# A transformer block on one core: filler matmuls between attention slots, and a new share of softmax tiles for VectorE

## The chip, the cores and the metric

The kernel runs on one core of one Trainium2 chip. The metric is the device time of one launch in microseconds (us), the median over several runs. A trace of one more execution, the profiled one, shows every instruction of the five engines: TensorE (PE, whose weight loads are listed apart as PEld), VectorE (DVE), ScalarE (ACT), GpSimd (POOL) and SyncE (SP, which here only issues DMAs).

## The reference

One pre-layernorm block over 2048 rows of width 640, in bf16: 32 heads of width 20, then a gated MLP of width 1728.

```python
h  = x + attention(layernorm(x), wqkv, wo)       # 32 heads, softmax over 2048 keys, scale 20**-0.5
n  = layernorm(h)
h2 = h + (gelu_tanh(n @ w_gate) * (n @ w_up)) @ w_down
```

## The kernel before

**Attention in tiles.** A tile is 128 x 512 scores in one bank of the sums' memory (eight banks of 512 f32). It comes from matmuls of 32 rows (line 965, `qk_mms`), is exponentiated, and goes into the output sums of its head through matmuls of 21 columns ("PV", built in `pv_op`, recorded under line 368 with `v_all` as an operand). Four tiles, one for each of four heads, are a *quad*. The queries are cut into eight chunks (`SIZES`: one of 512, five of 256, two of 128), and each chunk into *slots* of 64 tiles: 32 slots in all (0 to 7 for the first chunk, four for each chunk of 256, two for each of 128). All PV sums of a slot gather in bank 6. At the slot's end DVE copies them out (`osb`, line 1047, recorded under 368), four transposes (line 1057) and a few DVE operations finish them, and only after the copy may the next slot's first PV write to bank 6.

**Two engines make the exponentials.** Most tiles go to ACT, two or three tiles in one instruction (1024 or 1536 columns, written to `pts` or to `pts2`, which lies in `rege`). In each slot `D_QUADS` quads go to DVE instead (`d_exp`): one instruction at line 889 for each tile empties the bank into 16-bit integers, and a chain of five or six more (a polynomial in 16-bit arithmetic; a DMA that adds takes the place of one of them in most slots) works on two tiles at once before slot 18 ("narrow", 1024 columns) and on four from slot 18 = `D_WIDE` on ("wide", 2048 columns). `D_LEAD` says how many ACT tiles ahead of its place a DVE quad is begun; where it is zero (slots 0 to 8) the quads lie in the first `D_PART` of the slot.

**The rest is background.** The projections, and for each finished chunk the output projection, layernorm, gate (line 1138, emptied at 1173), GELU on ACT, up (1138 again, emptied at 1187) and down matmuls (1218, emptied at 1222) are placed wherever an engine is free. GELU and exp lie in different tables of ACT, so each group of GELUs between exps has a table load before and after it. The last chunk's part, after the last exp, is the *tail*.

**The order is made in advance.** All operations are recorded with an estimated duration, a priority and their dependencies; `Sched.schedule` plays them through once with these estimates, and each engine then runs its list strictly in the order that came out. An estimate that is changed moves operations in the lists; it changes no instruction. The scheduler also adds *filler matmuls* that compute nothing of use, when PE has nothing to do and its recent share of work falls under a bound (`WARM_MIN` of the last `WARM_WIN` = 3.4 us, `PAD_MIN` likewise). One filler kind multiplies zeros into bank 6 (four matmuls of 32 columns, `sc.pad`), possible before the change only while a slot's sums are being gathered (`live`). The other writes an idle bank (`sc.warm`, `self.spare`).

Of the kernel before, what the change touches and what calls it, by code (L numbers as in the profile page):

```python
# [18 lines left out]
WARM_WIN, WARM_MIN = 3.4, 0.5  # L19
# [27 lines left out]
class Sched:  # L47
# [13 lines left out]
    def op(self, eng, fns, dur, prio, reads=(), writes=(), acq=(), rel=(), after=(), sem=None, lat=None, mode=None, util=0.0):  # L61
        if eng == "dve" and rel and prio > self.ev:
            prio = self.ev
        o = Op()
        o.i = len(self.ops)
        o.eng, o.dur, o.lat, o.sem = eng, dur, DRAIN[eng] if lat is None else lat, sem
        o.util = util
        o.mode = mode
        o.tag = writes[0] if writes else None
        o.fns = fns if isinstance(fns, list) else [fns]  # L70
        o.prio = (prio, o.i)
        deps = set(after)
        for r in reads:
            if r in self.lw:
                deps.add(self.lw[r])
        for w in writes:
            if w in self.lw:
                deps.add(self.lw[w])
            deps.update(self.rd.get(w, ()))
        for r in reads:  # L80
            self.rd.setdefault(r, []).append(o.i)
        for w in writes:
            self.lw[w] = o.i
            self.rd[w] = []
        deps.discard(o.i)
        o.deps = deps
        o.acq = list(acq)
        o.rel = list(rel)
        o.succ = []
        o.ready = 0.0  # L90
        self.ops.append(o)
        return o.i

    def schedule(self):
# [5 lines left out]
        free_at = [0.0] * 8  # L100
        owner = [None] * 8
        last = [None] * 8
# [3 lines left out]
        mode = {e: None for e in ENGINES}  # L106
# [5 lines left out]
        order = []  # L112
        t = 0.0
        recent = collections.deque()
        live = False
        due = None
        total = len(ops)
        while done < total:
            assert events, "no operation can start"
            t = heapq.heappop(events)  # L120
            while events and events[0] <= t + 1e-9:
                heapq.heappop(events)
            for e in ENGINES:
                while future[e] and future[e][0][0] <= t + 1e-9:
                    _, p, i = heapq.heappop(future[e])
# [6 lines left out]
                while ready[e]:  # L132
                    p, i = heapq.heappop(ready[e])
                    o = ops[i]
# [40 lines left out]
                if chosen is None:  # L175
                    if e == "pe" and self.warm is not None:
                        while recent and recent[0][0] < t - WARM_WIN:
                            recent.popleft()
                        b = next((b for b in self.spare if owner[b] is None and free_at[b] <= t + 1e-9), None)
                        free7 = b is not None and all(hasattr(ops[d], "fin") and ops[d].fin + 0.06 <= t for d in self.warm_deps)  # L180
                        if sum(x for _, x in recent) < WARM_MIN * WARM_WIN and (free7 or live):
                            o = Op()
                            o.i, o.eng, o.lat = len(ops), "pe", DRAIN["pe"]
                            o.prio, o.sem, o.tag, o.util = (9, 0), None, "warm", 0.213
                            o.acq, o.rel, o.succ, o.dur = [], [], [], 0.215
                            if live and (mode[e] == "col" or not free7):
                                o.fns, o.mode, o.deps = list(self.pad), "col", set()
                            else:
                                o.fns, o.mode = [self.warm[b]], "full"
                                o.deps = set(self.warm_deps) | ({last[b]} if last[b] is not None else set())  # L190
                                last[b] = o.i
                            ops.append(o)
                            chosen = o
                            total += 1
                    if chosen is None:
                        continue
                o = chosen
                if e == "pe" and o.tag and o.tag[0] == "S":
                    self.spare = self.spares[o.tag[1]]
                if e == "pe" and self.pad is not None and o.tag and o.tag[0] in ("O", "OD"):  # L200
                    s_ = o.tag[1] if o.tag[0] == "O" else o.tag[1][0]
                    self.left[s_] -= 1
                    live = self.left[s_] > 0
                    while recent and recent[0][0] < t - PAD_WIN:
                        recent.popleft()
                    u = sum(x for _, x in recent) + o.util
                    room = due - t - MODE_SWITCH[e] if due is not None and due > t else 1e9
                    while u < PAD_MIN * PAD_WIN and o.util < 1.1 and o.dur + 0.215 < room and (live or o.tag[0] == "O"):
                        o.fns = o.fns + self.pad
                        o.dur += 0.215  # L210
                        o.util += 0.213
                        u += 0.213
# [120 lines left out]
DA_ISSUE, DA_LAT = 0.95, 7.0  # L333
DA_SLOTS = (1, 2, 3, 5) + tuple(range(9, 32))
PR, PR2 = 12, 6
D_QUADS = (1,) + (2,) * 15 + (2, 2) + (3,) * 10 + (2, 2, 2, 2)
D_FIRST, D_PART = 2, 0.75
D_LEAD = ((0,) * 8, (0, 10, 20) + (42,) * 21)
D_WIDE = 18
RSQRT_MAGIC = float(0x5F3759DF)  # L340

# [1 line left out]
P_QK, P_PV, P_PRO, P_EPI, P_LN, P_BG = 0, 1, 1.5, 2, 2.5, 3  # L343
# [3 lines left out]
def bass_sequential_preLN__mha_block__glu_gated_geglu__prompt_kernel(  # L347
# [12 lines left out]
    with ExitStack() as es:  # L360
        sc = Sched(nc)
        op = sc.op
# [4 lines left out]
        def I(method, *args, **kwargs):  # L367
            return lambda eng: getattr(eng, method)(*args, **kwargs)  # L368
# [64 lines left out]
        wg = carve(NA * DFF).rearrange("p (a f) -> p a f", a=NA)  # L433
        wu = carve(NA * DFF).rearrange("p (a f) -> p a f", a=NA)
# [55 lines left out]
        def cst(fn, key, n=128):  # L490
# [7 lines left out]
           reads=["zer"], writes=["qf1"])  # L498
        op("act", I("activation", f32(qt_all[:, 2, :, :]), zer[:, 0:2].bitcast(FP32).to_broadcast([128, 2048]), ACT.Copy), 1.8, P_QK,
           reads=["zer"], writes=["qf2"])  # L500
        op("act", I("activation", v_all[:, :, :, DH], zer[:, 0:1].unsqueeze(2).to_broadcast([128, NT, H]), ACT.Copy, bias=1.0), 0.5, P_QK,
           reads=["zer"], writes=["vones"])
# [28 lines left out]
        def load(dst, src, key, mb, after=(), writes=None):  # L531
            return op("sp", I("dma_start", dst, src), 0.08, P_BG, writes=writes or [key], after=after,
                      sem=key, lat=mb)
# [85 lines left out]
                   rel=[bk], after=after)  # L619

        def dma_transposes(src, rkeys, dst, wkey, after=()):
            op("sp", I("dma_start_transpose", dst, src), 1.25, P_EPI, reads=rkeys, writes=[wkey], sem=f"xp{wkey[1]}", lat=2.0, after=after)

        _id = [0]

# [182 lines left out]
        slot_end = []  # L808
        lead = sum(D_LEAD, ())
        for s_, (c, gs) in enumerate(slots):  # L810
            nk = 512 // CHUNKS[c][1]
            quads = [(s_, g, kb) for g in gs for kb in range(NT // nk)]
            n = D_QUADS[s_]
            taken = [quads[len(quads) * (m + 1) // (n + 1)] for m in range(n)]
# [432 lines left out]
        for s_, (c, gs) in enumerate(slots):  # L1247
            if c == 0:
                g = s_
                if g + 1 in STEP:  # L1250
                    t, (g0, g1) = g + 1, STEP[g + 1]
                    pr = P_EPI if t == 1 else P_BG
                    proj_q(t, 0, BG0, pr)
                    proj_k(t, BG0, pr)
                    q_bound(0, (t - 1, t), g0, g1, BG0, pr)
                if g < 3:
                    for kt in range(NT * g // 3, NT * (g + 1) // 3):
                        proj_v(kt, 1, BG0, P_BG)
                if g == 5:
                    prefetch(0)  # L1260
                if g >= 5:
                    cc = g - 4
                    for t in range(NA):
                        proj_q(t, cc, BG0, P_BG)
                    q_bound(cc, tuple(range(NA)), 0, NG, BG0, P_BG)
                if g == 7:
                    wr = tuple(w_readers)
                    load(wg, B_w_gate.rearrange("(a p) f -> p a f", p=128), "wg", 11.0, after=wr)
                    load(wu, B_w_up.rearrange("(a p) f -> p a f", p=128), "wu", 16.0, after=wr)
                    load(wd[:, 0:NF - 1, :], B_w_down[0:(NF - 1) * 128, :].rearrange("(a p) d -> p a d", p=128),  # L1270
                         "wd", 21.0, after=wr)
                    r0 = (NF - 1) * 128 - F0[-1]
                    load(wd[r0:128, NF - 1, :], B_w_down[(NF - 1) * 128:DFF, :], "wd", 2.6, after=wr)
                    op(POOL, I("memset", wd[0:r0, NF - 1, :], 0.0), 0.8, P_BG, writes=["wdz", "pool"], after=wr)
            while ui < len(units) and begins[ui] < slot_end[s_]:
                unit(ui)
                ui += 1
            if gs[-1] == NG - 1:
                tail = c == len(CHUNKS) - 1
                sc.ev = P_EV  # L1280
                post(c, ALLB if tail else BGF[c + 1], ALLB if tail else BGC[c + 1], tail)
                if not tail:
                    prefetch(c + 1)
# [30 lines left out]
```

## Time and profile before

| | us |
|---|---|
| median of 3 runs (915.36 to 915.76) | 915.65 |
| the profiled execution, whole | 915.13 |
| its span from the first to the last instruction | 913.0 |
| ACT busy | 871.2 |
| PE busy | 832.7 |
| DVE busy | 763.3 |
| POOL busy | 134.2 |

The 2.1 us between the profiled time and its span lie outside the trace, and that execution was 0.5 us faster than the median. Busy times are unions: neighbouring instructions of one engine overlap a little, so durations of single instructions add up to more. Instructions made through the helper in line 368 all carry that line, and are told apart by their tiles.

### The profile page before, as it was taken

What the parts mean: (1) busy time and instruction counts of PE and PEld (TensorE: products, weight loads), DVE (VectorE), ACT (ScalarE), POOL (GpSimd) and SP (SyncE); (2) the same over time, 40 slices, a digit from 0 to 9 for tenths busy, and PEclk for the clock granted to TensorE, in tenths of its full rate; (3) what the DMA queues carried; (4) which work ended last, traced back from release to release, by engine and by line L of the source; (5) the groups of instructions that cost most, each with busy time, mean ns of one, the idle gap of its engine ahead of it and who ended that gap; (6) DMA issues with size and microseconds to landing.
All of it is one profiled execution on the core that took longest, in us unless ns stands there. A gap on an engine that the chain in (4) does not pass through costs nothing.

```text
span 913.0 us, 25152 instructions
## 1 busy us (share of the span) xinstructions
PE 832.7 (91%) x11135; PEld 383.4 (42%) x11180; DVE 763.3 (84%) x1426; ACT 871.2 (95%) x786; POOL 134.2 (15%) x239
## 2 busy tenths in 40 slices
PE   3999999998897887899998989999999999999998
PEld 2432222222243332334443443344444445666667
DVE  8869989988798985777887989989999998958643
ACT  7999899999999999999999999999999999999971
POOL 5001110000013111111321101031102110203000
PEclk9999999999999999999999999999999999999999
DMA  7213344346304231242422324433353344314300
GB/s 259 84 31 79 79 87 108 96 96 203 127 1 76 48 59 24 48 68 59 91 51 50 64 39 85 91 62 71 78 107 62 70 81 98 47 26 85 56 9 23
DMA packets 52500, 68.05 MB, mean 75 GB/s; under 512 B 20892, under 2 KB 38392, under 8 KB 52392
## 3 DMA queue, kind: packets, MB, share of 16 engines
q0 software_dynamic: 12960, 33.56, 20.4%
q1 hardware_dynamic: 39432, 32.89, 13.2%
q8 instruction: 87, 1.43, 0.6%
q14 instruction: 21, 0.17, 0.1%
HBM read 20.12 MB, written 8.09 MB: 31 GB/s over the span
## 4 chain that ended last, share of the span: by engine, by line
ACT 68%; PE 19%; DVE 7%; DMA 2%; POOL 2%; issue 1%; SPq 0%
ACT pts L368 43%; ACT rege L368 24%; PE ps L965 5%; PE ps L667 4%; PE ps L1138 3%; PE ps L368 3%; PE ps L1218 3%; DMA regw<-in_A_wqkv_dram 1%; ACT L368 1%; DVE qt_all L368 1%; DVE rege L889 1%; DVE qt_all L889 1%; DVE dwx L368 1%; POOL nw L368 1%; DVE rege L368 1%
## 5 line engine op out<-in xcount | busy, mean ns | idle before, releaser
L368 ACT ACTIVATE pts<-ps 128x1536 bf16<-128x1536 f32 (+1 forms) x468 | 556.1, 1352 | 5.1 <-PE ps L965 2.7
L965 PE MATMUL ps<-qt_all,kt_all 32*128 32x256 bf16 (+2 forms) x4096 | 315.0, 274 | 42.6 <-ACT pts L368 25.5
L368 ACT ACTIVATE rege<-ps 128x1536 bf16<-128x1536 f32 (+1 forms) x232 | 289.7, 1359 | 5.5 <-PE ps L368 3.8
L965 PEld LDWEIGHTS ps<-qt_all,kt_all 32*128 32x128 bf16 x4096 | 108.6, 92 | 252.6 <-ACT pts L368 130.5
L1138 PE MATMUL ps<-rege,regw 128*128 128x256 bf16 (+2 forms) x1103 | 158.0, 274 | 9.6 <-DVE rege L1187 3.6
L368 PE MATMUL ps<-pts,v_all 128*21 128x256 bf16 (+2 forms) x2338 | 124.5, 276 | 0.4 <-ACT pts L368 0.3
L1138 PEld LDWEIGHTS ps<-rege,regw 128*128 128x128 bf16 x1120 | 85.9, 98 | 61.4 <-issue 27.0
L889 DVE TENSOR_SCALAR rege<-ps 128x512 int16<-128x512 f32 x120 | 82.3, 686 | 19.6 <-PE ps L965 18.7
L368 PE MATMUL ps<-rege,v_all 128*21 128x256 bf16 (+2 forms) x1358 | 91.8, 280 | 0.4 <-DVE rege L368 0.2
L889 DVE TENSOR_SCALAR qt_all<-ps 128x512 int16<-128x512 f32 x116 | 79.5, 686 | 12.0 <-PE ps L965 11.1
L667 PE MATMUL ps<-regw 128*128 128x512 bf16 (+1 forms) x345 | 84.2, 351 | 4.7 <-DMA regw<-in_A_wqkv_dram 1.6
L1218 PE MATMUL ps<-regw,rege 128*128 128x320 bf16 x448 | 78.1, 301 | 1.7 <-DVE rege L1222 0.8
L368 DVE TENSOR_TENSOR qt_all<-qt_all 128x2048 int16<-128x2048 f16 (+3 forms) x79 | 74.2, 940 | 1.0
L368 PEld LDWEIGHTS ps<-pts,v_all 128*21 128x21 bf16 x2338 | 53.9, 91 | 32.3 <-issue 26.9
L368 DVE TENSOR_SCALAR qt_all<-qt_all 128x2048 int16<-128x2048 int16 (+3 forms) x111 | 63.5, 574 | 1.0
L1187 DVE TENSOR_TENSOR rege<-rege,ps 128x512 bf16<-128x512 bf16 (+1 forms) x53 | 35.8, 678 | 23.7 <-PE ps L1138 21.8
L368 DVE TENSOR_TENSOR rege<-rege 128x1024 f16<-128x1024 f16 (+1 forms) x74 | 50.6, 684 | 0.9
L1218 PEld LDWEIGHTS ps<-regw,rege 128*128 128x128 bf16 x448 | 37.4, 97 | 30.5 <-issue 13.6
L368 DVE TENSOR_SCALAR rege<-rege 128x1024 int16<-128x1024 int16 (+2 forms) x112 | 48.3, 439 | 2.2 <-DMA rege<-qt_all 1.0
L368 PE MATMUL ps<-kt_all,zer 128*32 128x512 bf16 x576 | 49.5, 390 | 0.0
L667 PEld LDWEIGHTS ps<-regw 128*128 128x128 bf16 x360 | 28.1, 99 | 45.8 <-issue 24.4
L368 PEld LDWEIGHTS ps<-rege,v_all 128*21 128x21 bf16 x1358 | 36.0, 91 | 21.7 <-issue 14.2
(114 smaller groups left out, 785.4 us busy)
## 6 DMA issues: line engine op xcount, KB each, us to landing
qt_all<-qt_all POOLq DMA_DIRECT2D x11, 512.0 KB, 5.1
qt_all<-dwx POOLq DMA_DIRECT2D x11, 512.0 KB, 5.8
rege<-rege POOLq DMA_DIRECT2D x16, 256.0 KB, 3.6
rege<-dwx POOLq DMA_DIRECT2D x8, 512.0 KB, 5.3
dvx<-qt_all POOLq DMA_DIRECT2D x8, 512.0 KB, 4.6
rege<-in_A_x_dram SPq DMA_DIRECT2D x5, 640.0 KB, 5.8
q_rows<-regw SPq DMA_DIRECT2D x20, 128.0 KB, 1.9
out_dram<-rege SPq DMA_DIRECT2D x16, 160.0 KB, 2.6
```

The costliest lines, as they stand in the source:

```text
L368: return lambda eng: getattr(eng, method)(*args, **kwargs)
L667: yield op("pe", lambda eng, l=l, r=r, k=k: eng.matmul(bank(bk, n), l, r, start=(k == 0), stop=(k == len(steps) - 1)), c_mm(n) + cold, pri ...
L889: d_ops.append(op("dve", lambda eng: eng.tensor_scalar(v[:, 512 * h:512 * h + 512], bank(b), EXP_MUL, -32000.0, ALU.mult, ALU.max), c_dve( ...
L965: return lambda eng: eng.matmul(out()[:, kk * nq:(kk + 1) * nq], kt_all[32 * j:32 * j + 32, g, kt * 128:(kt + 1) * 128], qt_all[32 * j:32 ...
L1138: op("pe", lambda eng, a=a, f=f, fi=fi: eng.matmul(bank(bk)[:, fi * nq:(fi + 1) * nq], w[:, a, F0[f]:F0[f] + 128], hnT[:, a, 128 * tb:128 ...
L1187: hdone.append(op("dve", lambda eng, bu=bu, fv=fv, w=w: eng.tensor_tensor(fv, fv, bank(bu, w), ALU.mult), c_dve(w), p, reads=[ku] + hkeys( ...
L1218: op("pe", lambda eng, f=f, o=o, hf=hf, bk=bk: eng.matmul(bank(bk, 320), ha_f[:, o:o + 128], wd[:, f, hf * 320:(hf + 1) * 320], start=(f = ...
```

## The change

The zero matmuls may now also be placed between two slots, when bank 6 has been copied out and the next slot's first PV has not come (`free6`, after the first PV of the kernel, `begun`). The DVE quads are spread anew: three instead of two in slots 13 and 15; from slot 18 on a pattern of 3, 3, 2 in place of ten slots with three and four with two; 74 quads instead of 73. They are begun 36 tiles ahead instead of 42, and lie in the first 65% of the slots 0 to 8 instead of 75%. Three estimates of DMA times are longer: a transposing DMA 2.8 us for 2.0, the loads of the gate and up weights 12.0 and 17.5 us for 11.0 and 16.0.

```diff
-        live = False
+        live = begun = False
...
                         free7 = b is not None and all(hasattr(ops[d], "fin") and ops[d].fin + 0.06 <= t for d in self.warm_deps)
-                        if sum(x for _, x in recent) < WARM_MIN * WARM_WIN and (free7 or live):
+                        free6 = begun and not live and owner[6] is None and free_at[6] <= t + 1e-9
+                        if sum(x for _, x in recent) < WARM_MIN * WARM_WIN and (free7 or live or free6):
...
                             if live and (mode[e] == "col" or not free7):
                                 o.fns, o.mode, o.deps = list(self.pad), "col", set()
+                            elif free6 and (mode[e] == "col" or not free7):
+                                o.fns, o.mode, o.deps = list(self.pad), "col", {last[6]}
+                                last[6] = o.i
...
-                    live = self.left[s_] > 0
+                    live, begun = self.left[s_] > 0, True
...
-D_QUADS = (1,) + (2,) * 15 + (2, 2) + (3,) * 10 + (2, 2, 2, 2)
-D_FIRST, D_PART = 2, 0.75
-D_LEAD = ((0,) * 8, (0, 10, 20) + (42,) * 21)
+D_QUADS = (1,) + (2,) * 11 + (2, 3, 2, 3, 2, 2) + (3, 3, 2) * 3 + (3, 3, 2, 3, 2)
+D_FIRST, D_PART = 2, 0.65
+D_LEAD = ((0,) * 8, (0, 10, 20) + (36,) * 21)
...
         def dma_transposes(src, rkeys, dst, wkey, after=()):
-            op("sp", ..., 1.25, P_EPI, reads=rkeys, writes=[wkey], sem=f"xp{wkey[1]}", lat=2.0, after=after)
+            op("sp", ..., 1.25, P_EPI, reads=rkeys, writes=[wkey], sem=f"xp{wkey[1]}", lat=2.8, after=after)
...
-                    load(wg, ..., "wg", 11.0, after=wr)
-                    load(wu, ..., "wu", 16.0, after=wr)
+                    load(wg, ..., "wg", 12.0, after=wr)
+                    load(wu, ..., "wu", 17.5, after=wr)
```

In the changed file four lines are added ahead of most of the code, so line 368 becomes 372, 889 becomes 893, 965 becomes 969, 1138 becomes 1142, 1218 and 1222 become 1222 and 1226.

## The prediction

> **What bounds the kernel now.** I read the page first, then the clock and the engines in short stretches, ACT's own timeline with its idle times, and the chain of the last 50 us.
>
> ```profile
> PE 832.7 (91%) x11135; PEld 383.4 (42%) x11180; DVE 763.3 (84%) x1426; ACT 871.2 (95%) x786; POOL 134.2 (15%) x239
> ACT 68%; PE 19%; DVE 7%; DMA 2%; POOL 2%; issue 1%; SPq 0%
> ```
>
> ACT is busy 95% and holds 68% of the chain that ended last. Its timeline has no idle time worth naming between 40 and 876 us, except in a few places; these are the longest (idle time and releaser in brackets):
>
> ```profile
> 95.34 2.37 ACT L368 ACTIVATE rege<-ps 128x1536 bf16<-128x1536 f32 x2 [2.77 <-PE ps L368]
> ...
> 199.14 2.37 ACT L368 ACTIVATE rege<-ps 128x1536 bf16<-128x1536 f32 x2 [0.98 <-PE ps L368]
> ...
> 302.21 4.62 ACT L368 ACTIVATE pts<-ps 128x1536 bf16<-128x1536 f32 x4 [1.05 <-PE ps L368]
> 570.10 1.02 ACT L368 ACTIVATE pts<-ps 128x1024 bf16<-128x1024 f32 x1 [0.80 <-PE ps L965]
> 571.32 2.37 ACT L368 ACTIVATE pts<-ps 128x1536 bf16<-128x1536 f32 x2 [0.19 <-PE ps L965]
> 595.02 2.60 ACT L368 ACTIVATE rege<-ps 128x1536 bf16<-128x1536 f32 x2 [1.00 <-PE ps L965]
> 598.49 2.37 ACT L368 ACTIVATE pts<-ps 128x1536 bf16<-128x1536 f32 x2 [0.86 <-PE ps L965]
> ```
>
> The last four, 2.85 us, belong together. Cut into stretches of 2 us (columns: PE, PEld, DVE, ACT, POOL busy with counts, granted clock, DMA share, GB/s), the granted clock is 1.00 except here and, for 6.8 us, from 590.9:
>
> ```profile
> 564.00:566.00 2.00, 1.48 (x24) 0.54 (x22) 2.00 (x5) 2.00 (x3) 0.00 (x0) 1.00 0.00 0
> 566.00:568.00 2.00, 1.63 (x22) 0.82 (x22) 2.00 (x4) 2.00 (x3) 0.85 (x1) 0.75 0.03 8
> 568.00:570.00 2.00, 2.00 (x30) 0.60 (x18) 1.29 (x4) 1.30 (x1) 0.32 (x1) 0.50 0.67 131
> ```
>
> Both dips begin at the end of a slot (DVE copies `osb` at 564.44 and 591.18), after a stretch in which PE has almost only score matmuls. With half the clock PE falls behind ACT.
>
> After the last exp (876.3 us) the chain is PE's:
>
> ```profile
> 874.65 3.23 PE ps L1138 x32
> ...
> 894.78 3.81 PE ps L1218 x28
> 898.58 7.11 PE ps L1138 x127
> 905.69 0.02 issue
> 905.71 0.43 DVE rege L1163
> 906.14 0.05 issue
> 906.19 3.99 PE ps L1218 x28
> ```
>
> So there are two limits: ACT until 876 us, then, for 34 us, the matmuls that PE has left. A gain must take time from ACT before its last exp, or matmuls from behind it.
>
> **The change part by part.** The order of the changed program's instructions gives the counts; prices come from the rows of before.
>
> *ACT's own work.* Exps of 1024 columns fall from 344 to 342, those of 1536 stay at 356 (one more quad on DVE). A 3+2 pair of tiles repeats every 2.26 us; a third tile costs 1563 - 1139 = 424 ns; that leaves (2.26 - 0.42)/2 = 0.92 us for one of 1024. Gain 1.84 us. But the GELU of 1792 columns (chunk 6), which ran in the tail at 881.4 us for 1.70 us, now stands before the last exps, after another GELU group: +1.65. Net **-0.2** before the last exp. Table loads fall from 16 to 14, at 1.28 us each; both that vanish were in the tail, where ACT waits 1.6 to 5.6 us at a time for others: counted at nothing. If ACT were the tail's bound they would give 2.6.
>
> *Early slots, 65% for 75%.* A two-quad slot has 56 ACT tiles; the last DVE tile moves from 0.94 x 0.75 x 56 = 39 to 34 tiles, 5 tiles earlier, each 2.26/5 = 0.45 us: 2.4 us. The idle times at the ends of slots 1, 2 and 5 (2.77, 0.42, 0.21 and 0.98) come from there: the DVE copy of bank 6 stands behind chain work, the next slot's PV waits for the copy, and ACT for the score buffers that PV would free. Of these 4.4 us a shift of 2.4 would take 4.0 (2.4 off the first, the rest whole); but what moves forward meets other DVE work (22.8 us of 25 busy from 75 to 125), so the bound on the other side is nothing. I take the middle, **-2.2**.
>
> *Clock.* The changed order has 52 of its 620 zero matmuls between slots (none of 576 before), and 66 full-width ones for 62. Eleven more groups of four, 0.28 us each by 843.60 to 844.15 (eight in 0.55), are 3 us of PE, and four wide ones at 0.22 another 0.9. They go where PE waits: its weight loads wait 191 us in all for ACT to free a bank (130.5 and 60.9). So nothing on the path; without that cover, 3.9. If both dips go, 2.85 us return. But by columns times the share of the array they use, matmuls filled 0.45 of the 3.4 us before the first dip, and a dozen other such stretches at 0.45 or less kept the clock; a new order may dip elsewhere, at about 1.4 us a time. Two thirds: **-1.9**, bounds -2.85 and +1.4.
>
> The Trainium skill ("TensorE: Matmul & The Clock Gate", section "HAM oscillation — how this bites in real kernels") warns only of PE gaps of more than about 3.4 us; the trace halves the clock after waits of PE of at most 0.56 us, with PE busy 1.48 of 2.00 us. Here the trace decides; what the rule would make of the pads is the second rival.
>
> *DVE.* Two more narrow quads, one wide less. Narrow: 4 x 0.686 to empty the banks, two chains of 3 x 0.42 and 2 x 0.684: 8.0 us. Wide: 2.74 + 3 x 0.687 + 2 x 1.216 = 7.2. Net +8.8 us on 763, with three more adding DMAs on POOL's queue (about 0.9 us each of a POOL busy 15%). Slots 12 to 17 take it: by instruction lists times durations they go from 139 to 150 us of DVE work, against 148 us of ACT time; from slot 18 on the sum stays (352 and 354), but it no longer presses ten slots in a row, where DVE was busy 23.8 to 24.9 of each 25 us (600 to 750). Nothing for that as long as DVE's lateness stays inside the lead; two slot ends, 13 and 15, are newly full, and three patterns later: I allow **+1.5**, about two waits of the size of 0.66 and 1.05 seen at slot 9.
>
> *Lead 36 for 42.* Six tiles, 2.7 us less between a quad's start and its use. The last tile of a three-quad slot is begun 36 + 0.04 x 52 = 38 tiles, 17 us, before the slot ends; after it come 4.5 us of chain, about 5 us of adding DMA (4.6 to 5.8 for 512 KB), and queueing. Nothing, within those 7 us of slack; beyond them, the first rival.
>
> *The tail.* Behind the last score matmul stand 25 matmuls of 1138 with 256 columns fewer (all of them), 20 fewer of 128 columns (200 for 220), and 107 of 1218 for 112. Prices: 7.11/127 = 0.056, (3.23 - 7 x 0.056)/25 = 0.113, 3.9/28 = 0.14. 2.8 + 1.1 + 0.7 = 4.6 us, which PE does before the last exp instead; there its weight loads wait 11.4 us for ACT between 750 and 876 us, which hides it. What comes late next is DVE: between output projection and the last transposes PE had 23 + 46 matmuls of cover (5.7 us) and now has 20 + 25 (4.2), while the layernorm chain there took 5.3 us to its last instruction, 0.4 of it behind an emptying. At worst PE waits 1.3 us; at best two stops of 0.57 us behind line 1222 (880.5, 884.0) go too. Bounds -3.3 and -5.7; I take **-4.0**.
>
> *Longer estimates.* They only reorder; the transposing DMA took 3.3 us in the trace, the loads 10.7 and 15.7. SP issues 181 instructions before and after, and one store and one prefetch change places. Nothing.
>
> Sum: -0.2 - 2.2 - 1.9 + 1.5 - 4.0 = -6.8. Profiled 915.13 gives 908.3; the median stood 0.5 higher: **908.8 us**.
>
> **The rivals.** *Too short a lead (slower).* At a slot's end its last DVE quad is not ready, PE's queue stands at that PV, the copy and the next PVs follow, and ACT runs out of score buffers: the 2.77 us mechanism, now in slots 11 to 31. For it: 2.7 us less lead, and DVE near full there. Against: with 42, saturated DVE made hardly any such wait after slot 10. If half of the 21 slot ends pay the mean of the four slot-end waits (2.77, 0.42, 0.98, 1.05: 1.3 us), that is 14 us, in place of the allowance: 908.8 - 1.5 + 14 = 921. It decides from 8.3 us on, six such ends.
>
> *The clock does not follow the pads.* By the skill's rule they would buy nothing, since no gap of PE came near 3.4 us. The dips stay and one more comes: 908.8 + 1.9 + 0.7 (half a dip) = 911.4. For it: the dozen thin stretches that kept it show that padding is not the whole condition. Against: both dips lie exactly in unpadded slot ends.
>
> *The tail's gain is paid before it.* PE's extra background and pads in the last 125 us meet score matmuls; half of the 4.6 us returns as ACT idle time, and the early waits stay: 908.8 + 2.3 + 2.2 = 913.3, and with one dip more 914.7: no change.
>
> **How the numbers follow.** Chances: the forecast with its bounds (905 to 911) 0.42; better than that (early waits -4.0, clock -2.85, tail -5.7: 904.4) 0.10; clock 0.17; gain paid back 0.14, of which 0.08 lands within 0.2% (1.8 us, about what a measurement tells from no change); too short a lead 0.17. Faster: 0.42 + 0.10 + 0.17 + 0.06 = 0.75; same 0.08; slower 0.17. The range takes in all but the far end of the lead rival and the last of the good case: 903.5 to 917. The faster cases alone span 903.5 to 913.3.
>
> **What would show it.** Right: last exp ends near 873.5 us, span's end 32.7 us after it (36.7 before); granted clock 1.00 at slot ends; ACT idle after slots 1, 2 and 5 under 2 us in sum. Wrong: ACT idle times behind PE L372 (PV) after slot 12; half clock in other places; in the tail, PE waiting for DVE's layernorm operations before the last transposes.

## The result, and the profile after

The changed kernel takes **910.8 us** (median; 909.7 to 912.4) against 915.5 us for the kernel before beside it: a ratio of 0.9957, 95% interval 0.9942 to 0.9972. It is faster by 0.43%; the forecast was 908.8 us. In a later set of runs (experiment 5) the ratio was 0.9968 (0.9955 to 0.9980).

The profiled execution took 910.32 us, its span 908.4 us, 4.6 us less than before. From the page:

```profile
PE 831.5 (92%) x11183; PEld 386.0 (42%) x11228; DVE 768.4 (85%) x1445; ACT 867.3 (95%) x782; POOL 133.3 (15%) x242
ACT 55%; PE 28%; DVE 14%; POOL 3%; issue 1%; DVEq 0%
```

ACT's timeline, every start with a wait of 0.4 us or more between 45 and 880 us (bracket: idle time and releaser):

```profile
55.72 4.63 ACT L372 ACTIVATE pts<-ps 128x1536 bf16<-128x1536 f32 x4 [1.04 <-PE ps L372]
97.25 2.37 ACT L372 ACTIVATE rege<-ps 128x1536 bf16<-128x1536 f32 x2 [2.70 <-PE ps L372]
...
149.95 3.28 ACT L372 ACTIVATE pts<-ps 128x1024 bf16<-128x1024 f32 x3 [1.04 <-PE ps L372]
...
618.73 1.02 ACT L372 ACTIVATE pts<-ps 128x1024 bf16<-128x1024 f32 x1 [2.23 <-PE ps L372]
642.81 4.63 ACT L372 ACTIVATE pts<-ps 128x1536 bf16<-128x1536 f32 x4 [0.47 <-PE ps L372]
...
801.02 2.37 ACT L372 ACTIVATE pts<-ps 128x1536 bf16<-128x1536 f32 x2 [0.61 <-PE ps L969]
```

In this execution the two clock dips are gone. The same places, the ends of slots 19 (563.5) and 20 (589.2), in stretches of 2 us (PE, PEld, DVE, ACT, POOL, clock, DMA share, GB/s):

```profile
564.00:566.00 2.00, 1.98 (x30) 0.99 (x31) 0.82 (x2) 2.00 (x3) 0.00 (x0) 1.00 0.00 0
566.00:568.00 2.00, 2.00 (x35) 0.91 (x24) 0.59 (x3) 2.00 (x3) 0.00 (x0) 1.00 0.00 0
...
590.00:592.00 2.00, 1.98 (x30) 0.93 (x31) 2.00 (x4) 2.00 (x3) 0.00 (x0) 1.00 0.66 228
```

And the chain at the end, which is PE's again:

```profile
875.77 1.33 PE ps L1222 x9
877.10 0.56 PE ps L1142 x10
877.65 0.56 PE ps L372 x32
...
890.19 3.81 PE ps L1222 x28
893.99 7.11 PE ps L1142 x127
901.10 0.02 issue
901.12 0.43 DVE rege L1167
901.55 0.05 issue
901.60 3.99 PE ps L1222 x28
```

Where 32 matmuls of line 1138 stood between the last score matmul and the last PV, there are now 9 down matmuls and 10 of the gate or up kind with 128 columns. **Nothing was won before the last exp: it ends at 877.3 us, 1.05 us later than before. The whole gain lies behind it: 31.1 us to the end of the span, 36.7 before.** The waits of ACT of 0.15 us and more between exps sum to 9.9 us, before 9.8. The 2.85 us of the dips came back as other waits, first of all 2.23 us at the end of slot 21.

### The profile page after: what moved, and what is told of

The parts are those of the page before. It is cut to its first block, busy times and chain, and to the rows that moved or that the text cites. A ratio compares the mean times of both kernels' runs of the same rounds, so it can differ in the third digit from the quotient of the medians.

```text
span 908.4 us, 25274 instructions
## 1 busy us (share of the span) xinstructions
PE 831.5 (92%) x11183; PEld 386.0 (42%) x11228; DVE 768.4 (85%) x1445; ACT 867.3 (95%) x782; POOL 133.3 (15%) x242
## 4 chain that ended last, share of the span: by engine, by line
ACT 55%; PE 28%; DVE 14%; POOL 3%; issue 1%; DVEq 0%
ACT pts L372 34%; ACT rege L372 19%; PE ps L969 8%; PE ps L372 5%; PE ps L671 5%; PE ps L1142 5%; PE ps L1222 4%; DVE dwx L372 3%; DVE qt_all L372 2%; DVE rege L893 1%; DVE qt_all L893 1%; POOL nw L372 1%; DVE rege L1109 1%; ACT L372 1%; DVE stats L372 1%
## 5 line engine op out<-in xcount | busy, mean ns | idle before, releaser
L372 ACT ACTIVATE pts<-ps 128x1024 bf16<-128x1024 f32 (+1 forms) x467 | 552.9, 1330 | 7.0 <-PE ps L372 5.5
L969 PE MATMUL ps<-qt_all,kt_all 32*128 32x256 bf16 (+2 forms) x4096 | 314.2, 272 | 39.6 <-ACT pts L372 19.2
L372 ACT ACTIVATE rege<-ps 128x1024 bf16<-128x1024 f32 (+1 forms) x231 | 284.5, 1328 | 3.5 <-PE ps L372 3.1
L1142 PE MATMUL ps<-rege,regw 128*128 128x256 bf16 (+2 forms) x1101 | 154.5, 272 | 8.8 <-DVE rege L1191 3.6
L372 PE MATMUL ps<-pts,v_all 128*21 128x256 bf16 (+2 forms) x2330 | 122.0, 275 | 0.6 <-ACT rege L372 0.5
L893 DVE TENSOR_SCALAR rege<-ps 128x512 int16<-128x512 f32 x124 | 84.8, 686 | 15.6 <-PE ps L969 14.9
L372 DVE TENSOR_TENSOR qt_all<-qt_all 128x1024 int16<-128x1024 f16 (+3 forms) x81 | 74.7, 922 | 1.1
L372 PE MATMUL ps<-kt_all,zer 128*32 128x512 bf16 x620 | 54.8, 386 | 0.3 <-DVE osb L372 0.3
L372 POOL DMA_DIRECT2D qt_all<-dwx x25 | 23.0, 921 | 169.2 <-DVE dwx L372 158.6
```

The costliest lines, as they stand in the source:

```text
L893: d_ops.append(op("dve", lambda eng: eng.tensor_scalar(v[:, 512 * h:512 * h + 512], bank(b), EXP_MUL, -32000.0, ALU.mult, ALU.max), c_dve( ...
L969: return lambda eng: eng.matmul(out()[:, kk * nq:(kk + 1) * nq], kt_all[32 * j:32 * j + 32, g, kt * 128:(kt + 1) * 128], qt_all[32 * j:32 ...
L1142: op("pe", lambda eng, a=a, f=f, fi=fi: eng.matmul(bank(bk)[:, fi * nq:(fi + 1) * nq], w[:, a, F0[f]:F0[f] + 128], hnT[:, a, 128 * tb:128 ...
```

## The experiments

Each ran beside the kernel before on the same chip. "Tail" in the expectations is mostly the time from the last exp to the span's end. The table at the end of this section counts from the start of the last score matmul, which is the cleaner mark. "Waits" of ACT are those of 0.15 us and more.

**1. The same order, more matmuls behind it.** Is the tail only the sum of the matmuls left in it? The first matmul of each gate or up group of five is issued three times (the lines that fill `self.starts` are left out here).

```diff
+        end = max(n for n, o in enumerate(order) if o.tag and o.tag[0] in ("S", "SD"))
+        for o in order[end + 1:]:
+            if o.i in self.starts:
+                o.fns = [self.starts[o.i]] * 2 + o.fns
```

> The changed kernel with its order kept, and behind the last score matmul 80 matmuls of 128 columns added (the first of each gate or up group of five is done three times; the result is unchanged). If the tail is the sum of the matmuls PE has left there: 80 x 0.056 = +4.5 us, all of it behind the last exp (31.1 becomes 35.6 us), time about 915.3. If the tail is set by the chain of the last chunk's operations over DVE and ACT, PE takes them in waits: +0 to +1 us, about 911 to 912.

915.7 us, ratio to the kernel before 1.0005 (0.9984 to 1.0027): the gain is gone. The last score matmul is followed by 37.3 us, 32.8 in the changed kernel, and from the last exp the tail grew from 31.07 to 35.55: +4.5 both ways, against 4.5. The tail is PE's, matmul by matmul. At 127 matmuls of 128 columns in 7.11 us, each with its own weight load, one costs 0.056 us. The Trainium skill ("TensorE: Matmul & The Clock Gate", section "Back-to-back issue gap") gives about 81 ns for a stream of such pairs at 128 columns and about 56 ns by its formula for a single one; this stream runs at the second figure.

**2. The same order, thinner fillers between slots.**

```diff
                             elif free6 and (mode[e] == "col" or not free7):
-                                o.fns, o.mode, o.deps = list(self.pad), "col", {last[6]}
+                                o.fns, o.mode, o.deps = self.pad[:1], "col", {last[6]}
```

> The changed kernel with its order kept; of each group of four zero matmuls between slots only one is issued (13 instead of 52). If these fillers hold the clock: granted clock under 1.0 in most runs (about 0.996 for each dip of 3.4 us), a dip at one or more of the slot ends that lost them, +1.4 us for each, 912 to 914. If the clock does not follow them: clock and time as in the changed kernel, 910.8 (clock 1.0 in four of six runs there).

911.7 us, ratio 0.9971 (0.9948 to 0.9995), where the changed kernel had 0.9968 on that chip (experiment 5): three quarters of the zero matmuls between slots make no difference in time that these runs can tell. The granted clock does differ. It was under 1.0 in ten of the twelve runs, which the first theory expected; with all four matmuls of each group in the same order it was under 1.0 in seven of 23 (two of six and two of seven runs of the changed kernel, three of ten of experiment 1). So these fillers do seem to hold off some dips, but a dip is cheap: the 0.996 that the expectation gives to one dip of 3.4 us belongs to 6.8 us at half clock, and by experiment 5 each 3.4 us cost about 0.9 us. Where the dips fall is another matter: the profiled run had one of 3.4 us, at 798 us, and experiments 1 and 5 had one at 798 and 800 us too, with all four matmuls.

**3. The old estimates** for the transposing DMA and the two weight loads.

```diff
-            op("sp", ..., lat=2.8, after=after)
+            op("sp", ..., lat=2.0, after=after)
-                    load(wg, ..., "wg", 12.0, after=wr)
-                    load(wu, ..., "wu", 17.5, after=wr)
+                    load(wg, ..., "wg", 11.0, after=wr)
+                    load(wu, ..., "wu", 16.0, after=wr)
```

> The changed kernel with the three old DMA estimates (2.0, 11.0, 16.0 us), all else as changed. The order that comes out has 32 matmuls of 256 columns, 20 of 128 and 5 down matmuls more behind the last score matmul: 32 x 0.113 + 20 x 0.056 + 5 x 0.14 = 5.4 us, two table loads more, and the last chunk-6 GELU behind the last exp again. If the tail's matmuls made the gain: tail about 36.5 us, time 915 to 917. If the gain came from the quads and the fillers and the estimates are worth nothing: 910.8 +- 1.

922.9 us, ratio 1.0097 (1.0062 to 1.0132). The estimates that the prediction counted at nothing decide whether the change gains or loses. Up to 650 us the waits are those of the changed kernel to 0.02 us, apart from 0.6 us more around slot 9. Then comes another order, with 7.7 us of waits of ACT behind 650 us in the profiled run, where the changed kernel has 0.8 (two clock dips among their causes), and 39.3 us behind the last score matmul. The expectation, 915 to 917 us, came near on the tail (36.5 us from the last exp, 37.5 measured) and did not have those waits.

**4. No fillers between slots**, all else as changed.

```diff
-                        if sum(x for _, x in recent) < WARM_MIN * WARM_WIN and (free7 or live or free6):
+                        if sum(x for _, x in recent) < WARM_MIN * WARM_WIN and (free7 or live):
```

> The changed kernel without zero matmuls between slots (the condition as it was before), all else as changed; the order is made anew. Behind the last score matmul stand 39 matmuls of 256 columns, 20 of 128 and 5 down matmuls more: +6.2 us. Theory of the tail: tail 37.3 us, and with one or two clock dips 1.4 us each before it, 917 to 920. Theory that the fillers act through the clock alone: one or two dips, 912 to 914, tail 31 us.

920.9 us, ratio 1.0081 (1.0056 to 1.0107), 39.7 us behind the last score matmul, two dips (359 and 677 us); none of the nine runs had the full clock. With experiment 2 this says what the fillers do: as work for PE, in an order that is kept, they are worth so little time that it was not told apart from nothing; as operations in the list they move all that follows, and this order has the long tail.

**5. The changed kernel again.**

> The changed kernel itself, beside the next three on one chip. 910.8, last exp near 877.3 us, tail 31.1 us, and the same early waits (1.04, 2.70, 0.21, 1.04 us). A clock dip, where one comes, near 798 us, where the other two runs of this order had it.

911.0 us, ratio 0.9968. The profiled run shows the waits of the first one, 1.04, 2.70, 0.21, 1.04 and 2.23 us, to 0.01 us: they belong to the order. What differs are two dips, at 493 and 800 us: the wait at 495 us is 1.24 for 0.29, that at 803 us 1.70 for 0.61. This run's two dips make a granted clock of 0.996. In the first set of runs the two with 0.996 took 912.0 and 912.4 us, the four with 1.0 910.4 in the mean: 1.8 us for 6.8 us at half clock, about 0.9 for a dip of 3.4 us.

**6. The fillers alone**, in the kernel before: the whole `begun` and `free6` part of the diff, and nothing else of it.

> The kernel before with the fillers between slots and nothing else (68 zero matmuls there). Its order has the same tail within 0.2 us (31.05 against 30.83 us of matmuls). If the fillers hold the clock: no dip at the two slot ends that had one (567 and 591 us), 2.85 us less, about 912.9. If they only shuffle the order: dips elsewhere or in the same places, 915 +- 1.5 by the first chip's level, within 0.2% of the kernel before.

916.1 us, ratio 1.0027 (1.0013 to 1.0042): slower. The dips at 567 and 591 us are gone, and others stand elsewhere. The stretches of 2 us in this kernel:

```profile
740.00:742.00 2.00, 1.23 (x16) 0.34 (x14) 2.00 (x4) 2.00 (x3) 0.00 (x0) 0.95 0.00 0
742.00:744.00 2.00, 2.00 (x34) 0.71 (x26) 2.00 (x4) 1.61 (x2) 0.00 (x0) 0.50 0.00 0
...
862.00:864.00 2.00, 0.81 (x29) 0.40 (x17) 0.69 (x1) 2.00 (x2) 0.00 (x0) 1.00 0.95 183
864.00:866.00 2.00, 1.25 (x12) 1.25 (x13) 0.00 (x0) 1.97 (x3) 0.00 (x0) 0.67 0.01 0
```

Here the first dip follows a slice in which PE was busy 1.23 of 2.00 us, the second one a slice with 0.81. Neither expectation named a loss; it is a wait of 2.71 us at 875 us that came on top, after the second dip had ended: there PE's list has 30 gate or up matmuls (3.45 us from 871.41) ahead of the score matmuls that ACT waits for. The loss is not the dips': the three runs with the full clock took 915.3 us in the mean, two such runs of the kernel before 912.4.

**7. 75% again** in slots 0 to 8.

```diff
-D_FIRST, D_PART = 2, 0.65
+D_FIRST, D_PART = 2, 0.75
```

> The changed kernel with the DVE quads of slots 0 to 8 in the first 75% again. The tail has 39 matmuls of 256 columns, 10 of 128 and 5 down matmuls more: +5.7 us, tail 36.8 us, time about 916.5. Early waits: if the share of the slot sets them (the step of the prediction), up to 2.4 us more at each of slots 0, 1, 3 (7 us in sum against 5.0). If the planned delay of the adding DMA sets them (7 us for chains of two tiles, 3.3 to 3.6 in the traces), about the same 4.4 to 5.

919.4 us, ratio 1.0055 (1.0033 to 1.0076). The early waits are those of the kernel before (2.78, 0.41, 0.20, 0.98), 4.4 us in place of 5.0: for them 65% was no better than 75%. From the last score matmul to the end 38.9 us, as the count said; the tail counted from the last exp is only 32.6, since here a GELU and two table loads stand before the last two exps. From 498 us the clock stayed at half for 17 us, the longest dip seen, with 6.3 us of waits of ACT.

**8. A shorter planned delay** of the adding DMA.

```diff
-DA_ISSUE, DA_LAT = 0.95, 7.0
+DA_ISSUE, DA_LAT = 0.95, 5.5
```

> The changed kernel with the planned delay of the adding DMA 5.5 for 7.0 us (DA_LAT; the DMA is unchanged). If that delay holds back a slot's last PV in the order: the early waits at slots 0, 1 and 3 (1.04, 2.70, 1.04) fall by up to 1.5 each, to 1.2 in sum. If DVE is really late there: unchanged, 5. The tail has 3 down matmuls fewer, 0.4 us less. So 907 by the first, 910.4 by the second, if nothing later opens.

919.3 us, ratio 1.0063 (1.0046 to 1.0079). The wait after slot 1 falls from 2.70 to 1.87, but the end of slot 5 now waits 2.33: the early waits are 5.9 us in all. The planned delay moves them and does not remove them. Neither expectation came near the time: all waits of ACT together sum to 14.9 us (9.9 in the changed kernel), with two clock dips among their causes, and the last exp ends 7.1 us later. Its tail stands out in the table: fewest matmuls, yet 1.1 us longer than the changed kernel's. The chain there leaves PE:

```profile
893.15 0.50 DVE rege L1109
893.68 0.49 DVE stats L372
894.17 0.39 DVE rege L1226
894.56 0.40 DVE stats L372
894.96 0.59 DVE rege L1191
```

These are operations of the last chunk's layernorm with emptyings of banks between them; the chain stays on DVE for 3.9 us. It is the second limit of the tail that the prediction named, reached when PE has too little to cover it.

**9. The quads of before** in the changed kernel.

```diff
-D_QUADS = (1,) + (2,) * 11 + (2, 3, 2, 3, 2, 2) + (3, 3, 2) * 3 + (3, 3, 2, 3, 2)
+D_QUADS = (1,) + (2,) * 15 + (2, 2) + (3,) * 10 + (2, 2, 2, 2)
```

> The changed kernel with the quads of before (73; ten slots of three in a row), all else as changed. Its order has 21 matmuls of 256 columns, 20 of 128 and 5 down matmuls more behind the last score matmul: 4.2 us. Theory that the tail's matmuls carry the gain: 37.5 us from the last score matmul to the end (32.9 in the changed kernel), ACT one quad more (1.8 us), 915 to 918. Theory that the new spread of quads matters only through DVE's load: waits of ACT after slot 18 change, the tail does not: 911 to 913.

915.6 us, ratio 1.0018 (1.0006 to 1.0030), 38.2 us behind the last score matmul, a dip of 10 us at 498 us and a wait of 3.32 us at 648 us. So the spread, too, is needed for the short tail.

**10. 55%.**

```diff
-D_FIRST, D_PART = 2, 0.65
+D_FIRST, D_PART = 2, 0.55
```

> The changed kernel with the DVE quads of slots 0 to 8 in the first 55% (65% changed, 75% before); the tail's order is the same to the matmul (107 down, 200 of 128 columns), the GELU groups stand behind the same exps. If the share sets the early waits (they were 4.4 us at 75% and 5.0 at 65%, which speaks against it): 2 us or more less, 908 to 909. If the waits at the first slots' ends come from where the order puts each last PV: some slots better, some worse, 4 to 6 us, 910 to 912.

**906.35 us, ratio 0.9907 (0.9893 to 0.9921)**, better than both. ACT's timeline, all its waits from 45 to 300 us:

```profile
54.69 4.62 ACT L372 ACTIVATE pts<-ps 128x1536 bf16<-128x1536 f32 x4 [0.32 <-PE ps L372]
...
297.11 3.71 ACT L372 ACTIVATE pts<-ps 128x1536 bf16<-128x1536 f32 x3 [1.05 <-PE ps L372]
```

Of 5.0 us of early waits (slots 0 to 8) 0.3 are left; 1.05 us stand at the end of slot 9, where the changed kernel had 0.4. What moved is the link that the prediction named, DVE's copy of bank 6 at the end of slot 1. In the changed kernel and here:

```profile
95.85 0.68 DVE L372 COPY osb<-ps 128x512 f32<-128x512 f32 x1
```

```profile
90.22 0.68 DVE L372 COPY osb<-ps 128x512 f32<-128x512 f32 x1
```

Counted from the first exp (at 33.62 and 33.30 us in these two) the copy began after 61.1 us before the change (75%), 62.2 in the changed kernel (65%), 60.9 with 60% (experiment 11) and 56.9 here. So the share works, but not in proportion: 75, 65 and 60% leave 4.4, 5.0 and 4.4 us of early waits, 55% leaves 0.3. Why the order steps between 60 and 55% is open (experiment 11 changes one estimate as well). From slot 10 on the run has the changed kernel's waits, 2.23 us at slot 21 among them, and two more, 1.14 us behind a clock dip at 353 us and 0.40 at 591 us; 32.8 us stand behind the last score matmul.

**11. 60% and 3.1 us for the transposing DMA.**

```diff
-D_FIRST, D_PART = 2, 0.65
+D_FIRST, D_PART = 2, 0.60
-            op("sp", ..., lat=2.8, after=after)
+            op("sp", ..., lat=3.1, after=after)
```

> A version made to be better: 60% and a transposing DMA estimated at 3.1 us (3.3 measured). The order has 108 down matmuls and 200 of 128 columns behind the last score matmul, so the same short tail (32.9 + 0.1 us). By the tail alone 911; better only if the waits of ACT before it (10 us in the changed kernel) happen to be fewer; 908 to 913.

909.9 us, ratio 0.9941 (0.9925 to 0.9957), 33.0 us behind the last score matmul. The early waits (1.04, 1.49, 1.88) are as long as before; the profiled run had three dips.

**12. One quad out of slot 21**, on top of experiment 10.

```diff
-D_QUADS = ... + (3, 3, 2) * 3 + (3, 3, 2, 3, 2)
+D_QUADS = ... + (3, 3, 2, 2, 3, 2) + (3, 3, 3) + (3, 3, 2, 3, 2)
```

> The 55% version with one DVE quad moved from slot 21 to slot 26 (still 74). Behind the last score matmul 108 down and 200 matmuls of 128 columns: the same tail, 32.9 us from the last score matmul. If the wait of 2.23 us at the end of slot 21 (in every run of the changed spread so far but the two whose orders differed before it) is a third DVE quad that comes late: it goes, nothing as long appears at slot 26's end, 904 (906.35 - 2.2). If a full DVE list is late wherever three quads meet background work: a wait of 1 to 3 us at another slot end, 905 to 908.

**904.3 us, ratio 0.9889 (0.9872 to 0.9905)**, the best kernel here. ACT's timeline from 480 to 700 us:

```profile
489.68 2.36 ACT L372 ACTIVATE pts<-ps 128x1536 bf16<-128x1536 f32 x2 [0.29 <-PE ps L969]
529.88 3.28 ACT L372 ACTIVATE pts<-ps 128x1024 bf16<-128x1024 f32 x3 [0.25 <-PE ps L372]
608.65 2.37 ACT L372 ACTIVATE pts<-ps 128x1536 bf16<-128x1536 f32 x2 [0.70 <-PE ps L969]
694.43 4.72 ACT L372 ACTIVATE pts<-ps 128x1536 bf16<-128x1536 f32 x4 [0.20 <-PE ps L969]
```

The 2.23 us are gone, and slot 26's end shows no wait in their place. From the last score matmul to the end it takes 33.8 us where 32.9 was expected: behind 20 matmuls of the gate or up kind PE stops for 0.77 us for an emptying on DVE (line 1191, at 881.39 us). That a third quad that comes late made it fits; the order around it changed as well, so the quad itself is not isolated.

**The tail in all of them.** "Matmuls" is their sum behind the last score matmul at the prediction's prices (0.113, 0.056 and 0.14 us for gate or up with 256 and 128 columns, and down); the rest (PV, transposes, output projection, the last copy and store) is the same in all.

| kernel | matmuls, us | last score matmul to span's end, us |
|---|---|---|
| before | 30.8 | 38.5 |
| changed (its run, experiment 5) | 26.2 | 32.8, 32.8 |
| 1 repeated matmuls | 30.7 | 37.3 |
| 2 thin fillers | 26.2 | 32.8 |
| 3 old estimates | 31.6 | 39.3 |
| 4 no fillers between slots | 32.4 | 39.7 |
| 6 fillers alone | 31.1 | 38.2 |
| 7 75% | 31.9 | 38.9 |
| 8 shorter DMA delay | 25.8 | 34.0 |
| 9 quads of before | 30.4 | 38.2 |
| 10 55% | 26.2 | 32.8 |
| 11 60%, 3.1 us | 26.3 | 33.0 |
| 12 quad moved | 26.3 | 33.8 |

The difference is 6.6 to 8.2 us throughout. There are two kinds of order, with about 26 and about 31 us of matmuls, and taking back any one of the four parts tried from the changed kernel (experiments 3, 4, 7, 9) leads to the long kind.

## Why the prediction was right, and where it was not

The direction, the size within a factor of two (4.7 us for 6.7) and the place of the largest term were right. That the sum came so near is in part luck: against the forecast the early slots came out 2.8 us worse, the new waits 0.9, ACT's start and own work 1.1, while clock and tail came out 0.9 and 1.6 us better. Term by term, in the profiled runs:

- **ACT's own work, -0.2:** about +0.1. The last exp ends 1.05 us later; 0.19 of that are more waits and 0.77 a later start of the exps (41.02 for 40.25 us behind the same wait). Other runs of this order started them between 39.6 and 40.7 us, so that 0.77 is one run's luck.
- **Early slots, -2.2:** measured +0.6. This is the step that failed. A shift of 2.4 us was taken off each wait; but the order changed with the share, and the copy at the end of slot 1 came 1.1 us later, not 2.4 earlier. Slot 1's wait stayed at 2.70 and new ones of 1.04 us came in slots 0 and 3. Experiments 7 and 10 show that the share acts on these waits, at slot 1 through that copy, with nothing gained at 65 and 4.1 us at 55% (0.3 left of the 4.4 before).
- **Clock, -1.9:** -2.85 in this execution; how much of it is the fillers' doing stays open. For the second rival: fillers alone leave dips in other places (experiment 6), and the profiled run of experiment 4, which has none between slots, keeps its clock at the ends of slots 19 and 20. Against it: in one order, thin fillers went with a clock under 1.0 in ten of twelve runs, full ones in seven of 23 (experiment 2). The price of a dip elsewhere, 1.4 us, was the mean of a dip of 3.4 and one of 6.8 us (0.99 and 1.86 us of waits); for 3.4 us the runs give about 0.9.
- **Allowance for new waits, +1.5:** mis-sized. After slot 12 the waits other than the dips' are 4.1 us for 0.3; 2.23 of them stand at the end of slot 21, a slot with three quads, in the way of the first rival (ACT behind PV). It happened at one slot end at that size, not at half of them. Against that, 1.3 us at slot 9 fell away, which nothing had foreseen.
- **Tail, -4.0:** -5.6, near its bound. 4.65 are the matmuls that were counted; the two stops behind line 1222 went as well (0.57 us each), and the layernorm chain on DVE did not come late: its last instruction began at 887.02 and the transposes at 887.62, behind 25 matmuls that had kept PE busy.
- **Longer estimates, nothing:** wrong as a statement on cause. It did no harm to the number, since the tail had been counted from the changed order itself. Experiment 3 shows that without them the short tail is gone and the time is 12 us longer.
- **DVE +8.8 us:** 5.1 by busy time, which is a union, where the prediction added single durations that overlap. **Lead 36 for 42:** not tried alone; with 42 the new spread needs more chain buffers than the kernel has.

Of the marks set beforehand: the clock stood at 1.00 at the slot ends in question, and PE did not wait for DVE's layernorm before the last transposes. But ACT's idle time after slots 1, 2 and 5 was 2.9 us where under 2 was asked for, and a wait behind PV after slot 12 appeared. The last exp was expected at 873.5 us with 32.7 us behind it; it was 877.3 and 31.1.

## What to carry to other kernels

Where a list scheduler fixes each engine's order, a change of an estimate or a filler is a change of everything behind it: read the order that comes out, count what stands behind the last instruction of the bounding engine, and price that; in experiment 1 that price held within 0.1 us, and over all kernels here what else stands there took 6.6 to 8.2 us. What happens ahead of that point is decided by a few waits, each of which can be found in the bounding engine's own timeline and sometimes moved by one parameter. Not every move pays: experiment 8 only shifted the waits elsewhere. Two such moves (55%, one quad out of slot 21) gave 6 to 7 us more than the change itself (ratios to the kernel before of 0.9889 for 0.9957 and 0.9968). And take parts back one at a time before crediting any of them: here each of the four tried was needed for the short tail, and the fillers, meant as work that holds the clock, mattered for the order that came out with them.

## What the runs showed of the hardware

The granted clock halved for 3.4, 6.8, 10.2 and 17.1 us at a time without any long gap of PE: in the 7 us ahead of a dip the longest was 1.6 us (experiment 3, at 836 us), in 16 of the 20 dips under 1 us. In experiment 7 PE counted as busy 4.00 of each 4.00 us while the clock stayed at half, here in slices of 4 us:

```profile
500.00:504.00 4.00, 4.00 (x44) 1.50 (x44) 3.49 (x5) 2.98 (x4) 0.00 (x0) 0.50 0.01 4
504.00:508.00 4.00, 4.00 (x38) 0.98 (x30) 2.46 (x4) 2.43 (x3) 0.85 (x1) 0.50 0.15 29
```

The Trainium skill ("TensorE: Matmul & The Clock Gate", section "HAM oscillation — how this bites in real kernels") ties the loss of clock to PE gaps of some 3.4 us; the section "A second HAM failure mode: psum-queue depth-cycling" ties it, in one other kernel, to frequent short ones between groups of matmuls. These traces do not agree with the first; the slices ahead of the dips of experiment 6 are not against the second. Nor did the clock in experiment 7 return after about 3.4 us of sustained matmuls, as the section "What's actually happening" of the same page of the Trainium skill describes it; but PE's work there was mostly matmuls of 32 rows or of 21 to 32 columns, and no run here shows whether such work counts in full. Between executions of one program the dips come and go at the same places (493 and 798 to 800 us in the changed order) while the waits that belong to the order repeat to 0.02 us. What exactly decides a dip stays open.
